# New costs for the planner that orders the engines of an attention and two feed-forward layers

## The chip, the core and the metric

One NeuronCore of a Trainium2 chip runs the whole program; nothing is shared with other cores. The metric is the device time of one execution in microseconds (us). The kernel before takes 1226.68 us, the median of three executions (1225.52 to 1226.89).

## What is computed

```python
q_s = softmax(q, axis=-1);  k_s = softmax(k, axis=2)     # 4 x 8 heads x 576 x 64
kv  = einsum('bhsd,bhse->bhde', k_s, v)
x   = einsum('bhsd,bhde->bhse', q_s, kv)                 # then 2304 tokens x 512
h   = x @ w_in                                           # 512 x 2048
x   = (h * clip(h + 3, 0, 6) / 6) @ w_out                # 2048 x 512
p   = domain_probs / (domain_probs.sum(-1) + 1e-9)       # 4 experts
out = sum over e of p[:, e] * (relu(x @ w1[e]) @ w2[e])  # 512 x 1024 x 512
```

Inputs and output are float32.

## The kernel before

**Attention.** There are four batches. `k_part` (lines 384 to 433) treats two heads at a time: K is loaded (L386) and V (L388), VectorE takes the maximum (L417), ScalarE the exponential (L419), TensorE transposes (L398) and multiplies (L405), VectorE scales the result into `bd` (L412, L413). `q_part` treats 128 tokens of Q at a time: load (L444), maximum (L462), a subtraction (`each`, recorded at L315), exponential (L465), sum (L467), reciprocal (L471), a multiplication (L315 again), four transposes on TensorE (L460). `x_part` makes the attention's result: a product (L499) into one of the PSUM places "pa", a copy of it, rounded to fp32r, by ScalarE (L502), and the rest of that rounding by VectorE (L506). There are 32 such products and 32 such splits, eight a batch. From the second batch on only two "pa" places may be used.

**First layer.** 96 steps, each with twelve matmuls of 384 columns (L606 to L608, called here a first product) and twelve more (L650, a second product). A step pairs one block of 384 tokens with one of 16 chunks of the hidden layer. Its result goes through ScalarE (L620), VectorE (L623), ScalarE (L629) and a subtraction that leaves the low half (L315, on VectorE or GpSimd). The chunks' weights arrive as float64 (L544); `w_half` turns each half of a chunk into a high and a low fp32r half: VectorE (L554), ScalarE (L558), VectorE twice (L560, L563), ScalarE (L566), VectorE (L569), a product of 512 columns (L315, `o6`), ScalarE (L574), a subtraction of 512 columns (L315, `o8`).

**Later layers.** `w_prepare` (L799 and L315, 256 columns) forms the second feed-forward layer's seven combinations of each weight block while the first layer runs and stores them to DRAM. Then come the three units of 768 tokens: the first at L1062 and L1184, the other two at L941 and L1257 with evictions at L1306.

**What sets the order.** The kernel emits nothing directly. Each operation is an `Op` with the engines that may run it and a cost on each; `Plan.order` (from line 155) plays the program through with these costs, engine by engine, takes at each time the ready operation with the smallest key, and the operations are emitted in the order of the starts so found. Each engine then runs its own list strictly in order on the chip. So a cost in the program changes no instruction; it changes where the instruction stands in its engine's list, and, where two engines may run it, on which. L315 is the helper `tt`, through which VectorE (DVE) and GpSimd (POOL) run the same `tensor_tensor`:

```python
def tt(o, out, a, b, op):
    on(o).tensor_tensor(out=out, in0=a, in1=b, op=op)
def rather_pool(n):
    return {"Pool": pool_(n), "DVE": dve2(n)}
```

The first engine of such a pair is preferred; the other takes the operation if the first would end it `PREFER = 1.5` us or more from now (for VectorE as the first: later than the other would).

Of the kernel before, what the change touches and what calls it, by code (L numbers as in the profile page):

```python
# [20 lines left out]
DM = H * D  # L21
# [3 lines left out]
P = 128  # L25
# [62 lines left out]


def dve2(n):  # L90

    return 0.155 + 1.6e-3 * n


def act(n):
    return 0.165 + 0.87e-3 * n


def pool_(n):
    return 0.2 + 2.4e-3 * n  # L100
# [5 lines left out]

# [19 lines left out]
class Plan:  # L126
# [23 lines left out]
    @staticmethod  # L150
    def after(e, x):
        to = next(iter(x.eng))
        return 0.0 if to == e else hop(e, to)

    def order(self):
# [5 lines left out]
        for o in reversed(self.ops):  # L161
            if o.due is None:
                e = next(iter(o.eng))
                o.due = min((x.due - self.after(e, x) for x in o.then), default=1e6) - o.eng[e]
# [4 lines left out]
        clock = dict.fromkeys(engines, 0.0)  # L169
# [10 lines left out]
        done, t, total = [], 0.0, len(self.ops)  # L180
        while len(done) < total:
            moved = False
            soon = [c for c in clock.values() if c > t]
            for e in engines:
# [3 lines left out]
                for o in cand[e]:  # L188
# [4 lines left out]
                    if best is not None and o.key >= best.key:  # L193
                        continue
# [41 lines left out]
def tile_kernel(ctx: ExitStack, tc: tile.TileContext, q, kt, v, w64, w, p, out):  # L236
# [147 lines left out]
    def k_part(b, j):  # L384
        pst = {}
        ld = load("kt", {"SP": 0.85}, lambda o: nc.sync.dma_start(out=KT[o.place], in_=kt[b, j]),  # L386
                  (), ("kt", lambda n: b < 3 or n < 3))
        vld = load("v", {"SP": 0.95}, lambda o: nc.sync.dma_start(out=V[o.place], in_=v[b, j]),  # L388
# [28 lines left out]
        o1 = add({"DVE": 0.74}, lambda o: nc.vector.tensor_reduce(  # L417
            out=nms[ld.place], in_=t(), axis=AX.X, op=ALU.max, negate=True), [ld])
        o2 = add({"ACT": 0.77}, lambda o: nc.scalar.activation(  # L419
            out=t(), in_=t(), func=AF.Exp, bias=nms[ld.place]), [o1])  # L420
        to = load("ek", {"": 0.0}, lambda o: None, [o1], ("ek", lambda n: n < 2 or b == 0))
        o3 = add({"PE": 0.85}, lambda o: turn(o, range(4)), [o2, to], pa_place(b == 0))
        o5 = add({"PE": 0.2}, lambda o: turn(o, [4]), [o3], pa_place(b == 0), [("kt", ld)])
        o4 = add({"ACT": 0.6}, lambda o: nc.scalar.activation(
            out=EK[to.place][:, 0:4 * P], in_=pst[o3], func=AF.Copy), [o3], None, [("pa", o3)])
        o6 = add({"ACT": 0.26, "DVE": 0.28}, lambda o: copy(
            o, EK[to.place][:D, 4 * P:5 * P], pst[o5][:D, :]), [o5, o4], None, [("pa", o5)])
        o7 = add({"PE": 1.2}, kv, [o6, vld] + bd_readers[j], pa_place(b == 0),
                 [("ek", to), ("v", vld)])
        o8 = add({"DVE": 0.5}, scale, [o7], None, [("pa", o7)])  # L430
# [10 lines left out]
    def q_part(b, t):  # L441
        n = min(P, S - t * P)
        pst = {}
        ld = load("q", {"SP": 0.75}, lambda o: nc.sync.dma_start(  # L444
# [17 lines left out]
        o1 = add({"DVE": 0.67}, lambda o: nc.vector.tensor_reduce(  # L462
            out=m(), in_=heads(x()), axis=AX.X, op=ALU.max), [ld])
        o2 = add({"Pool": 1.2, "DVE": 0.7}, lambda o: each(o, ALU.subtract), [o1])
        o3 = add({"ACT": 0.62}, lambda o: nc.scalar.activation(  # L465
            out=x(), in_=x(), func=AF.Exp), [o2])
        o4 = add({"DVE": 0.67}, lambda o: nc.vector.tensor_reduce(  # L467
            out=m(), in_=heads(x()), axis=AX.X, op=ALU.add), [o3])
        o4 = add({"ACT": 0.2}, lambda o: nc.scalar.activation(
            out=m(), in_=m(), func=AF.Copy, bias=EPS), [o4])  # L470
        o4 = add({"DVE": 0.18}, lambda o: nc.vector.reciprocal(m(), m()), [o4])  # L471
        o5 = add({"Pool": 1.25, "DVE": 0.7}, lambda o: each(o, ALU.mult), [o4])
        before = [o for s0, s1, bb, o in qt_readers if s0 < t * P + n and s1 > t * P and bb < b]
        o6 = add({"PE": 0.8}, turn, [o5] + before, pa_place(b == 0 and t < 2), [("q", ld)])
        q_done[b, t] = add({"ACT": 0.6}, lambda o: nc.scalar.activation(
# [8 lines left out]
    def x_part(b, s0, n):  # L484
# [4 lines left out]
        for j in range(NPAIR):  # L489
            if (bi, j) not in x0_place:  # L490
                def new(o, j=j):
                    x0[bi, j] = x_tile(o.place, f"x0_{bi}{j}")

                x0_place[bi, j] = load("x", {"": 0.0}, new, (), ("x", None))
# [1008 lines left out]
```

## Time and profile before

| | |
|---|---|
| median of three executions | 1226.68 us |
| span of the profiled execution (the page has no other time of it) | 1225.2 us, 1.5 below the median |
| TensorE (PE) busy | 1196.2 us, 98% |
| TensorE weight loads (PEld) | 1148.9 us, 94% |
| VectorE (DVE) | 881.0 us, 72%, 1486 instructions |
| ScalarE (ACT) | 596.4 us, 49% |
| GpSimd (POOL) | 670.7 us, 55%, 656 instructions |
| HBM | 194 GB/s over the span |

The busy share of TensorE is the time in which some matmul is in flight, so it says when the engine stood still, and not whether it ran at its full rate. That is told by how many matmuls it gets through and by the granted clock.

### The profile page before, as it was taken

The page shows a single profiled execution, that of the slowest core. Times are in us where ns is not written, and L with a number is a line of the kernel's source. Part 1 is how long each engine was busy: PE and PEld are TensorE (multiplying, and loading weights), DVE is VectorE, ACT ScalarE, POOL GpSimd, SP SyncE. Part 2 cuts the span into 40 slices and gives each one's busy share as a digit, 9 for nine tenths or more (in the row PEclk, how much of TensorE's full clock was granted, in tenths as well). Part 3 has the DMA queues.
Part 4 walks back from the last instruction along what each step waited for, and adds up shares of the span by engine and source line. Part 5 has one row for each costly group of instructions (what it writes and reads, how often), then busy time and mean ns, then how long its engine had stood idle before and what let it go on. Part 6 is the DMA issues. An engine that isn't in the chain of part 4 may idle for free.

```text
span 1225.2 us, 21162 instructions
## 1 busy us (share of the span) xinstructions
PE 1196.2 (98%) x7296; PEld 1148.9 (94%) x7296; DVE 881.0 (72%) x1486; ACT 596.4 (49%) x1256; POOL 670.7 (55%) x656
## 2 busy tenths in 40 slices
PE   5799999999999999999999999999999999999998
PEld 4698999999999999988888899999999999999998
DVE  7889732888984866765665586777777877777775
ACT  6677433655654644544444444444444444444441
POOL 3767234756776865756666544444444654444442
PEclk9899999999999999999999999999999999999999
DMA  8433212345565653655555457787877788877771
GB/s 299 152 99 136 75 69 96 107 160 157 187 226 179 224 190 121 206 190 189 189 189 183 170 173 251 265 251 248 252 248 248 239 295 248 250 249 243 246 252 53
DMA packets 125275, 238.99 MB, mean 195 GB/s; under 512 B 14064, under 2 KB 14064, under 8 KB 125168
## 3 DMA queue, kind: packets, MB, share of 16 engines
q1 hardware_dynamic: 125168, 237.64, 59.1%
q8 instruction: 58, 0.95, 0.3%
q14 instruction: 49, 0.40, 0.1%
HBM read 174.14 MB, written 63.44 MB: 194 GB/s over the span
## 4 chain that ended last, share of the span: by engine, by line
PE 84%; DVE 5%; POOL 4%; issue 2%; DMA 2%; ACT 1%; SPq 0%; DVEq 0%; POOLq 0%; ACTq 0%
PE ps L1257 19%; PE ps L941 18%; PE ps L650 12%; PE ps L1184 11%; PE ps L1062 10%; PE ps L608 4%; PE ps L607 4%; PE ps L606 4%; POOL w L315 1%; PE ps L405 1%; POOL st L315 1%; DMA st<-in_w_dram 1%; DMA vd<-w 1%; PE ps L499 1%; DVE acc L1306 1%
## 5 line engine op out<-in xcount | busy, mean ns | idle before, releaser
L941 PE MATMUL ps<-x,w 128*128 128x384 f32 x1344 | 264.4, 335 | 0.0
L1257 PE MATMUL ps<-w,g 128*128 128x256 f32 x1737 | 244.2, 283 | 2.0 <-DVE acc L1306 1.8
L1257 PEld LDWEIGHTS ps<-w,g 128*128 128x128 f32 x1737 | 228.5, 189 | 6.0 <-DVE acc L1306 6.0
L941 PEld LDWEIGHTS ps<-x,w 128*128 128x128 f32 x1344 | 227.2, 189 | 0.8
L650 PE MATMUL ps<-g,w 128*128 128x384 f32 x1152 | 225.3, 340 | 1.8 <-ACT g L629 0.8
L650 PEld LDWEIGHTS ps<-g,w 128*128 128x128 f32 x1152 | 199.8, 188 | 7.0 <-DVE g L315 2.2
L1306 DVE SCALAR_TENSOR_TENSOR acc<-ps,pt,acc 128x256 f32<-128x256 f32 x312 | 143.4, 480 | 79.5 <-PE ps L1257 77.5
L315 POOL TENSOR_TENSOR w<-st,w 128x256 fp32r<-128x256 f32 (+1 forms) x133 | 137.3, 1048 | 99.6 <-ACT w L899 59.4
L315 POOL TENSOR_TENSOR g<-t,g 128x384 fp32r<-128x384 f32 x98 | 107.8, 1106 | 116.5 <-ACT g L964 114.3
L1184 PE MATMUL ps<-w,g 128*128 128x512 f32 x576 | 148.9, 394 | 0.0
L608 PE MATMUL ps<-x,w 128*128 128x384 f32 x384 | 129.4, 337 | 2.4 <-POOL w L315 1.8
L1062 PE MATMUL ps<-x,w 128*128 128x384 f32 x672 | 131.0, 335 | 0.0
L606 PE MATMUL ps<-x,w 128*128 128x384 f32 x384 | 129.1, 336 | 0.0
L607 PE MATMUL ps<-x,w 128*128 128x384 f32 x384 | 129.0, 336 | 0.0
L1062 PEld LDWEIGHTS ps<-x,w 128*128 128x128 f32 x672 | 119.4, 188 | 7.8
L1184 PEld LDWEIGHTS ps<-w,g 128*128 128x128 f32 x576 | 106.6, 188 | 16.7
L623 DVE SCALAR_TENSOR_TENSOR r<-r,ps 128x384 f32<-128x384 f32 x96 | 52.6, 549 | 76.5 <-ACT r L620 75.8
L620 ACT ACTIVATE r<-ps,three 128x384 f32<-128x384 f32 x96 | 55.7, 580 | 105.0 <-PE ps L608 103.0
L964 ACT ACTIVATE g<-t 128x384 fp32r<-128x384 f32 x145 | 73.8, 521 | 43.0 <-DVE t L1006 18.0
L949 ACT ACTIVATE t<-ps 128x384 f32<-128x384 f32 x90 | 44.1, 490 | 69.8 <-PE ps L941 69.6
L315 POOL TENSOR_TENSOR st<-st 128x256 f32<-128x256 f32 (+1 forms) x56 | 63.2, 1131 | 24.1 <-DVE st L569 20.3
L608 PEld LDWEIGHTS ps<-x,w 128*128 128x128 f32 x384 | 72.6, 189 | 3.3 <-POOL w L315 2.6
(173 smaller groups left out, 1932.0 us busy)
## 6 DMA issues: line engine op xcount, KB each, us to landing
w<-wd SPq DMA_DIRECT2D x224, 256.0 KB, 3.2
w<-vd SPq DMA_DIRECT2D x224, 256.0 KB, 3.6
vd<-w SPq DMA_DIRECT2D x112, 256.0 KB, 2.4
wd<-w SPq DMA_DIRECT2D x112, 256.0 KB, 3.3
st<-in_w_dram SPq DMA_DIRECT2D x64, 256.0 KB, 3.9
st<-in_w_dram SPq DMA_DIRECT2D x30, 512.0 KB, 3.9
raw<-in_w_dram SPq DMA_DIRECT2D x32, 256.0 KB, 3.5
out_dram<-acc SPq DMA_DIRECT2D x18, 256.0 KB, 2.3
```

Of the source, the lines that this page charges most:

```text
L315: on(o).tensor_tensor(out=out, in0=a, in1=b, op=op)
L606: nc.tensor.matmul(pst[0], lhsT=hi, rhs=a, start=(k == 0), stop=False)
L607: nc.tensor.matmul(pst[0], lhsT=hi, rhs=b, start=False, stop=False)
L608: nc.tensor.matmul(pst[0], lhsT=lo, rhs=a, start=False, stop=(k == NK - 1))
L620: nc.scalar.activation(out=pst["r"], in_=pst[0], func=AF.Relu, bias=three)
L650: nc.tensor.matmul(y, lhsT=l, rhs=r, start=(s["start"] and not low and m == 0), stop=(s["stop"] and bool(low)))
L941: nc.tensor.matmul(bank(i), lhsT=l, rhs=r, start=(opens and k == 0 and m == 0), stop=(k == 1 and m == 2), skip_group_check=not opens)
L964: nc.scalar.activation(out=made[i][0][:, :n], in_=at(src), func=AF.Relu if raw else AF.Copy)
L1062: nc.tensor.matmul(bank(i), lhsT=l, rhs=r, start=(opens and k == 0 and m == 0), stop=(k == 1 and m == 2), skip_group_check=not opens)
L1184: nc.tensor.matmul(y, lhsT=l, rhs=rr, start=opens and x == 0, stop=closes and x == len(seq) - 1)
L1257: nc.tensor.matmul(y, lhsT=l, rhs=r, start=clears and x == 0, stop=x == len(seq) - 1, skip_group_check=True)
L1306: o1 = add({"DVE": dve(half) + 0.03}, lambda o: nc.vector.scalar_tensor_tensor(out=a, in0=y, scalar=s, in1=a, op0=ALU.mult, op1=ALU.add), ...
```

## The change

Every cost that the planner uses is replaced. A cost is now a `Cost`: the time for which the engine is taken (the number itself), the time after which the result is there (`lat`), and whether the operation needs the SBUF port that VectorE and GpSimd share (`port`). The planner keeps one clock for this port: an operation with `port` is not started while another holds it. Loads cost their size over 400 KB per us and land 1.9 us later, instead of a fixed time each and 2.5 us. The hops between engines become shorter (0.05 to 0.09 us in place of 0.16 to 0.27). All engines start at 5.6 us, the load queue at 2.0 us.

```diff
-START, FIRST, COLD = 18.0, 0.75, 0.0
+START, FIRST, BEGIN = 18.0, 2.0, 5.6
+HOPS = {"PE": 0.06, "ACT": 0.05, "DVE": 0.05, "Pool": 0.09, "SP": 0.05, "": 0.0}
+LAND = 1.9
+class Cost(float):
+    def __new__(cls, occ, late=0.08, port=False):
+        x = float.__new__(cls, occ)
+        x.lat, x.port = occ + late, port
+        return x
 def hop(a, b):
-    if b == "SP":
-        return 2.0
-    return 0.27 if b == "PE" else 0.2 if a == "PE" else 2.5 if a == "SP" else 0.16
+    return LAND if a == "SP" else HOPS[b]
 def dve(n):
-    return 0.155 + 1.05e-3 * n
+    return Cost(0.064 + n / 960)
+def dvep(n):
+    return Cost(0.124 + n / 960)
 def dve2(n):
-    return 0.155 + 1.6e-3 * n
+    return Cost(0.064 + n / 960, 0.08, True)
 def act(n):
-    return 0.165 + 0.87e-3 * n
+    return Cost(0.092 + n / 1200, 0.1)
 def pool_(n):
-    return 0.2 + 2.4e-3 * n
+    return Cost(0.16 + 2.1e-3 * n if n < 600 else 3.25e-3 * n, 0.05, True)
+def dma(n):
+    return Cost(n / 400.0, 0.0)
...
@@ Plan.order
-        clock = dict.fromkeys(engines, 0.0)
+        clock = dict.fromkeys(engines, BEGIN)
...
+                    if o.eng[e].port and port > t:
+                        soon.append(port)
+                        continue
...
-                cold = 2 if e == "PE" and o.start < COLD else 1
-                clock[e] = o.start + o.eng[e] * cold
-                o.end = clock[e]
+                clock[e] = o.start + o.eng[e]
+                o.end = o.start + o.eng[e].lat
+                if o.eng[e].port:
+                    port = clock[e]
...
@@ w_half (the other operations likewise)
-        o1 = add({"DVE": 0.6}, lambda o: nc.vector.tensor_scalar(
+        o1 = add({"DVE": Cost(0.33, 0.08, True)}, lambda o: nc.vector.tensor_scalar(
...
-        o6 = add({"Pool": 1.35, "DVE": 0.7}, lambda o: tt(
+        o6 = add({"Pool": pool_(DM), "DVE": dve2(DM)}, lambda o: tt(
```

No instruction is added or taken out. By the lists of the built programs, 133 of the `tensor_tensor` instructions of L315 go from VectorE to GpSimd (58 of 256 columns, 47 of 384, 28 of 512) and 9 of 768 columns go the other way. TensorE's list differs up to the end of the attention and over some 190 matmuls at the end of the first layer; between and after these it is the same, row for row.

The next three places are those at which the lists differ and TensorE waits or is waited for. Names with a number are tiles; the changed file's lines are 32 further down, so that L347 there is L315 here.

TensorE, from the end of the first product of the first step (the first of all; `x_03` is the last of its operands, `ident` marks transposes, `qt` and `bd` the attention's products L499, `vs` and `spare_110` hold V, `g` is the operand of a second product). Before:

```order
L608 MATMUL ps_115<-x_03_143,w_0_1_145 128x384
L398 MATMUL ps_118<-ident,spare_109 64x128
L460 MATMUL ps_117<-ident,qs_97 128x128 x4
L460 MATMUL ps_118<-ident,qs_98 128x128 x4
L499 MATMUL ps_117<-qt,bd_91 128x192
L499 MATMUL ps_118<-qt,bd_89 128x192
L650 MATMUL ps_119<-g,w_1_0_146 128x384
L650 MATMUL ps_119<-g,w_1_1_147 128x384
```

After:

```order
L640 MATMUL ps_115<-x_03_152,w_0_1_148 128x384
L492 MATMUL ps_118<-ident,qs_97 128x128 x4
L492 MATMUL ps_117<-ident,qs_98 128x128 x4
L531 MATMUL ps_118<-qt,bd_91 128x192
L531 MATMUL ps_117<-qt,bd_89 128x192
L437 MATMUL ps_118<-vs_95,acc 128x129 x5
L531 MATMUL ps_117<-qt,bd_92 128x192
L531 MATMUL ps_118<-qt,bd_91 128x192
L437 MATMUL ps_117<-vs_96,acc 128x129 x5
L531 MATMUL ps_118<-qt,bd_90 128x192
```

The second product of the first step stood behind two products of the attention; now most of the second batch, and a part of the third, stands between.

VectorE, from the maximum or split that follows the first batch's last wide split to the first L569 (the last VectorE step of the first half chunk, whose operand is `st_113`). Before:

```order
L506 TENSOR_TENSOR x_03_143<-ps_122,x_03_143 128x384
L462 TENSOR_REDUCE qm_105<-qs_98 128x8
L417 TENSOR_REDUCE nm_100<-acc 128x1
L417 TENSOR_REDUCE nm_101<-acc 128x1
L506 TENSOR_TENSOR x_10_156<-ps_118,x_10_156 128x192
L417 TENSOR_REDUCE nm_102<-acc 128x1
L417 TENSOR_REDUCE nm_103<-spare_109 128x1
L560 SCALAR_TENSOR_TENSOR st_114<-st_114 128x512
L554 TENSOR_SCALAR acc<-acc 128x512
L467 TENSOR_REDUCE qm_104<-qs_97 128x8
L467 TENSOR_REDUCE qm_105<-qs_98 128x8
L569 SCALAR_TENSOR_TENSOR st_113<-st_113 128x512
```

After:

```order
L538 TENSOR_TENSOR x_03_152<-ps_122,x_03_152 128x384
L344 COPY acc<-ps_117 64x128
L494 TENSOR_REDUCE qm_106<-qs_99 128x8
L601 SCALAR_TENSOR_TENSOR st_113<-st_113 128x512
L592 SCALAR_TENSOR_TENSOR st_114<-st_114 128x512
```

The four maxima of K (L417) now stand further up, and steps of the next half chunks (`st_114`, `acc`) further down, so that the first L569 comes eight rows sooner behind the split.

GpSimd, around the same half chunk's last two operations (`st_113` is `o6`, `w_0_1_145` or `w_0_1_148` is `o8`; `qs` and `spare` are Q). Before:

```order
L315 TENSOR_TENSOR st_113<-st_113 128x512
L315 TENSOR_TENSOR qs_97<-qs_97,qm_104 128x512
L315 TENSOR_TENSOR qs_98<-qs_98,qm_105 128x512
L315 TENSOR_TENSOR w_0_1_145<-st_113,w_0_0_144 128x512
L315 TENSOR_TENSOR st_114<-st_114 128x512
L315 TENSOR_TENSOR w_1_1_147<-st_114,w_1_0_146 128x512
```

After:

```order
L347 TENSOR_TENSOR st_113<-st_113 128x512
L347 TENSOR_TENSOR qs_99<-qs_99,qm_106 128x512
L347 TENSOR_TENSOR qs_97<-qs_97,qm_104 128x512
L347 TENSOR_TENSOR w_0_1_148<-st_113,w_0_0_146 128x512
L347 TENSOR_TENSOR qs_98<-qs_98,qm_105 128x512
L347 TENSOR_TENSOR spare_111<-spare_111,qm_107 128x512
```

Between `o6` and `o8` stand two operations of Q in both; the second half's pair, which followed at once, now stands behind the rest of the second batch's Q.

The load queue's first thirteen loads are the same. After them the second batch's K comes ahead of its Q.

## Rows read from the trace of the kernel before

**Rows 1.** The page: the span.

```profile
span 1225.2 us, 21162 instructions
```

**Rows 2.** Windows by stage: stretch, its length, busy us and (instructions) by engine, clock, DMA share, GB/s.

```profile
0.00:66.00 66.00, 46.50 (x240) 39.22 (x241) 53.12 (x108) 41.20 (x87) 38.26 (x38) 0.90 0.66 217
66.00:150.00 84.00, 82.85 (x512) 76.87 (x511) 72.60 (x144) 55.61 (x116) 43.85 (x34) 1.00 0.33 107
...
225.00:350.00 125.00, 124.18 (x711) 122.61 (x710) 113.33 (x163) 71.67 (x143) 83.03 (x77) 1.00 0.51 165
...
730.00:1200.00 470.00, 468.75 (x3256) 463.06 (x3255) 349.67 (x625) 204.01 (x416) 224.62 (x208) 1.00 0.78 248
```

**Rows 3.** Timeline of PE: start us, length us, instruction, [idle before <-releaser].

```profile
14.52 0.60 PE L398 MATMUL ps<-ident,acc 128*128 128x128 f32 x4
14.96 0.60 PE L398 MATMUL ps<-ident,spare 128*128 128x128 f32 x4
...
17.06 1.28 PE L405 MATMUL ps<-spare,acc 128*128 128x129 f32 x10
18.17 1.28 PE L405 MATMUL ps<-vs,acc 128*128 128x129 f32 x10
...
23.06 2.85 PE L499 MATMUL ps<-qt,bd 128*128 128x384 f32 x8 [0.69 <-ACT qt L475]
25.75 0.99 PE L460 MATMUL ps<-ident,spare 128*128 128x128 f32 x8
...
41.73 0.45 PE L606 MATMUL ps<-x,w 128*128 128x384 f32 x1
...
163.20 0.81 PE L499 MATMUL ps<-qt,bd 128*128 128x384 f32 x2
```

**Rows 4.** The chain that ended last: start us, length us, piece; one second product.

```profile
166.61 2.08 PE ps L650 x12
```

**Rows 5.** Windows of 2 and 7.2 us at the start, as in rows 2.

```profile
28.00:30.00 2.00, 0.23 (x2) 0.03 (x1) 2.00 (x5) 1.57 (x4) 1.04 (x1) 1.00 0.82 264
33.40:40.60 7.20, 6.22 (x26) 5.38 (x26) 4.15 (x12) 3.40 (x10) 5.16 (x4) 0.50 0.54 167
```

**Rows 6.** Timeline of DVE, columns as in rows 3.

```profile
26.21 1.47 DVE L506 TENSOR_TENSOR x<-ps,x 128x384 fp32r<-128x384 f32 x3
...
33.22 0.68 DVE L569 SCALAR_TENSOR_TENSOR st<-st 128x512 f32<-128x512 uint32 x1
...
43.22 0.41 DVE L554 TENSOR_SCALAR st<-st 128x512 int32<-128x512 int32 x1
43.55 0.70 DVE L569 SCALAR_TENSOR_TENSOR acc<-acc 128x512 f32<-128x512 uint32 x1
...
48.44 1.53 DVE L563 TENSOR_SCALAR st<-st 128x512 int32<-128x512 int32 x1
...
55.29 0.68 DVE L462 TENSOR_REDUCE qm<-spare 128x8 f32<-128x512 f32 x1
55.88 0.35 DVE L506 TENSOR_TENSOR x<-ps,x 128x192 fp32r<-128x192 f32 x1
...
78.90 1.01 DVE L506 TENSOR_TENSOR x<-ps,x 128x384 fp32r<-128x384 f32 x2
```

**Rows 7.** Timeline of POOL, columns as in rows 3.

```profile
48.20 1.49 POOL L315 TENSOR_TENSOR w<-acc,w 128x512 fp32r<-128x512 f32 x1
...
61.13 1.31 POOL L315 TENSOR_TENSOR st<-st 128x512 f32<-128x512 f32 x1
...
169.42 0.74 POOL L315 TENSOR_TENSOR w<-raw,w 128x256 fp32r<-128x256 f32 x1
```

**Rows 8.** Groups of DVE from 225 to 350 us: xcount | busy us, mean ns | idle before.

```profile
L315 DVE TENSOR_TENSOR w<-st,w 128x512 fp32r<-128x512 f32 x5 | 6.9, 1384 | 1.1 <-ACT w L574 0.9
L315 DVE TENSOR_TENSOR w<-wtmp,w 128x256 fp32r<-128x256 f32 x7 | 6.3, 907 | 0.3 <-ACT w L799 0.3
L315 DVE TENSOR_TENSOR st<-st 128x512 f32<-128x512 f32 x3 | 3.9, 1305 | 0.0
```

More of the change, by code (lines that the diff above doesn't have):

```diff
@@ L152, in after @@
         to = next(iter(x.eng))
-        return 0.0 if to == e else hop(e, to)
+        if to == e and e in ("PE", "SP"):
+            return -0.165 if e == "PE" else 0.0
+        return hop(e, to)
     def order(self):
@@ L163, in order @@
                 e = next(iter(o.eng))
-                o.due = min((x.due - self.after(e, x) for x in o.then), default=1e6) - o.eng[e]
+                o.due = min((x.due - self.after(e, x) for x in o.then), default=1e6) - o.eng[e].lat
             if o.key is None:
@@ L179, in order @@
                 open_(o)
-        done, t, total = [], 0.0, len(self.ops)
+        done, t, total, port = [], 0.0, len(self.ops), 0.0
         while len(done) < total:
@@ L492, in new @@
                     x0[bi, j] = x_tile(o.place, f"x0_{bi}{j}")
-                x0_place[bi, j] = load("x", {"": 0.0}, new, (), ("x", None))
+                x0_place[bi, j] = load("x", NONE, new, (), ("x", None))
             pst = {}
@@ L507, in low @@
                                         in1=x[:, at:at + n].bitcast(F32), op=ALU.subtract)
[L509 removed]
+            o1 = add({"PE": pes(0.013 + 1.667e-3 * n)}, product, deps + [kv_done[b, j], x0_place[bi, j]],
                      pa_place(b == 0 and s0 == 0))
@@ L524, in new @@
             store[key] = w_tile(o.place, "w_" + "_".join(str(x) for x in key))
-        return load(kind, {"": 0.0}, new, (), (kind, None))
+        return load(kind, NONE, new, (), (kind, None))
     w0, w_done, w_place = {}, {}, {}
@@ L575, in w_half @@
             out=w0[c, i, 0], in_=t(F32), func=AF.Copy), [o6] + space)
-        o8 = add({"Pool": 1.35, "DVE": 0.7}, lambda o: half_sub(
+        o8 = add({"Pool": pool_(DM), "DVE": dve2(DM)}, lambda o: half_sub(
             o, w0[c, i, 1], t(F32), w0[c, i, 0]), [o7], None, [("wt", o1)])
@@ L610, in h_part @@
         deps = x_done[bi] if s["first"] else []
-        o0 = add({"PE": 12 * pe(n)}, product, deps + w_done[c][:1] + h_before, ("ph", None),
+        o0 = add({"PE": pes(12 * pe(n))}, product, deps + w_done[c][:1] + h_before, ("ph", None),
                  key=i - 1.0, due=s["due"])
@@ L910, in main_pe @@
     def main_pe(cost, fn, deps, take=None, give=()):
-        o = add({"PE": cost}, fn, deps + main["last"], take, give, due=main["due"])
+        o = add({"PE": pes(cost)}, fn, deps + main["last"], take, give, due=main["due"])
         o.key = o.due
@@ L1148, in low @@
                     op0=ALU.max, op1=ALU.subtract)
-            o2 = add({"DVE": dve(n)}, low, [o1], None, [("t", src)])
+            o2 = add({"DVE": dve2(n)}, low, [o1], None, [("t", src)])
             made[key] += [o1, o2, pl]
@@ L1319, in shares @@
     def shares():
-        ld = add({"SP": 0.6}, lambda o: nc.sync.dma_start(out=pt, in_=p))
+        ld = add({"SP": dma(36)}, lambda o: nc.sync.dma_start(out=pt, in_=p))
         def normal(o):
@@ L1330, in normal @@
             )
-        norm.append(add({"DVE": 1.0}, normal, [ld]))
+        norm.append(add({"DVE": Cost(1.0)}, normal, [ld]))
     for b in range(B):
@@ L1429, in tile_kernel @@
         if u == 0:
-            add({"": 0.0}, lambda o: None, stage0, None, [("xt", i) for i in range(2)])
-            add({"": 0.0}, g_of_stage, stage0, None, [("g", 200), ("g", 201)])
+            add(NONE, lambda o: None, stage0, None, [("xt", i) for i in range(2)])
+            add(NONE, g_of_stage, stage0, None, [("g", 200), ("g", 201)])
         if u + 1 < len(UNITS):
```

132 lines of the change are left out of this document (68 added, 64 removed).

## The prediction

> **What bounds the kernel now.** I read the page first, then windows by stage, then the timelines of TensorE (PE), VectorE (DVE) and GpSimd (POOL) in the first 165 us. The span is 1225.2 us [rows 1], 1.5 below the median of the runs, 1226.7. The windows [rows 2] show two kernels: up to 66 us PE is in use for 46.5 of 66 us at a mean granted clock of 0.90, and DVE for 53.1; from 66 us on PE never stands still for more than about one us in a hundred. So all that a new order can win at once lies in the first stretch, and the later stretches are a list of matmuls at their full rate that the change leaves as it is.
>
> To say how much lies there I compare PE's clock time with the work that it has done by then, at full rate. The rates: a transpose 0.11 us (four in 0.44, from 14.52 to 14.96), the five matmuls of one K and V product 1.11 (17.06 to 18.17), a product of the attention of 384 columns 0.67 (two records of 0.336, from 23.06 to 25.75), one of 192 columns half of that [rows 3], twelve matmuls of the first layer 2.08 [rows 4]. The attention as a whole is 160 x 0.11 + 16 x 1.11 + 16 x 0.67 + 16 x 0.34 = 51.6 us.
>
> - The first first-layer product starts at 41.73 us [rows 3]; ahead of it lie 60 transposes, six K and V products and six of the attention's, 16.7 us. PE is 25 us behind.
> - The last product of the attention starts at 163.20 [rows 3]; ahead of it in PE's list lie the attention less this product, 50.9, and 441 first-layer matmuls, 76.4: 127.3 us. PE is 35.9 us behind. Since PE is idle for only 1.2 us from 66 to 150 at a clock of 1.00 [rows 2], nearly all of this was lost before 66.
>
> What holds PE there is DVE. Back to back its instructions take less than their records say: a reduction 0.59 (55.29 to 55.88), an L554 0.33 (43.22 to 43.55), a wide split 0.47 [rows 6]. By such times, 0.66 for a maximum of K and 0.60 for L560 and L569, I add up DVE's list: 17.8 us up to the fourth split, 24.1 up to the first L569, 52.9 up to the sixteenth split. They end at 27.68, 33.90 and 79.91 [rows 6]. So DVE is 9.9, 9.8 and 27.0 us later than its bare work: some 10 us of start and waits for loads, and 17 more later on. Where those go the rows show: an L554 or L563 that takes 0.41 alone takes 1.53 at 48.44, while GpSimd is in the middle of an operation (48.20, 1.49 long, which takes 1.31 elsewhere) [rows 6, 7]. Each of the two engines makes the other wait. 38 of the 128 DVE instructions up to the sixteenth split are of this kind.
>
> **The change part by part.** *Engines.* 133 `tensor_tensor` go from DVE to POOL and nine of 768 columns come back. On POOL one takes 1.31 us (512 columns) or 0.74 (256) alone [rows 7]. In the first stretch this cover is there: POOL is in use for 38.3 of 66 us [rows 2].
>
> *DVE's list.* Up to the sixteenth split it now holds 116 instructions, 46.1 us by the same times: twelve more reductions and maxima, seven fewer evictions, and 17 instead of 38 that contend for the port. Up to the first L569 it holds 20.5 us instead of 24.1. With the same 9.8 on top this L569 ends at 30.3 instead of 33.9, and the first first-layer product can start some 4 to 6 us sooner, at about 36: on POOL the same two Q operations stand between the half chunk's two.
>
> *PE's list.* Ahead of the second first product stood 18.2 us of attention and now stand 29.5, so that the attention comes earlier and fewer products of the first layer are there to fill its waits. Up to the second first product PE now has 94 transposes, ten K and V products, 16 of the attention's products and two twelves: 10.3 + 11.1 + 8.1 + 4.2 = 33.7 us. It stands behind the sixteenth split: the last product's place must be free, then two K and V products and four transposes follow, 2.7 us, of which some 1.0 passes while ScalarE and DVE still drain that product. So it starts 1.7 us after the sixteenth split ends.
>
> *The unknown* is how late DVE then is against its 46.1 us. Low end: 9.8, as at the first L569, nothing being added. High end: 27.0, as now. Between the first L569 and the sixteenth split the 17.2 us were added over 28 instructions of the contending kind, 0.61 each; 12 are left there, 7.3 us, which makes 17.1. I take 15, since part of the 17.2 was DVE idling behind first-layer products that no longer stand there (eight evictions, now one). Then the split ends at 61.1, the second first product starts at 62.8, and PE is 62.8 - 33.7 = 29.1 us behind. From there to the attention's end DVE has 41.3 us of bare work against 54.7 of PE's, so I add only 1.5 us, about the idle time of 66 to 150 now. PE ends the attention 30.6 us behind, not 35.9.
>
> *Loads.* Their number and the first thirteen are the same; the second batch's K before its Q agrees with DVE's list, so I cost it at nothing. If a load were late there DVE would stand with it; bounds are zero and the 2 to 3 us between issue and landing that the early rows leave.
>
> *After the attention.* PE's list is the same but for a swap at the end of the first layer. PE's own idle time there is 0.8 us in 225 to 350 and 1.3 in 730 to 1200 [rows 2]: that much can be won, and I take zero.
>
> **Sum:** 1225.2 - 35.9 + 30.6 = 1219.9 us of span, and with the 1.5 around it **1221.4 us**.
>
> **A rule that speaks against it.** Where the trace has both engines at work, the second to come waits for all of the first [rows 6, 7], and an operation holds the other engine off longer on POOL (0.74 or 1.31) than DVE's own time for it. From 225 to 350 us, DVE is in use for 113.3 of 125 and POOL for 83.0 [rows 2]. Five L315 of 512 columns into `w`, three into `st` and seven of 256 columns out of `wtmp` run on DVE there [rows 8]; with three single ones, eight of 512 and ten of 256 go to POOL. On DVE they hold the port for about 8 x 0.60 + 10 x 0.33 = 8.1 us, on POOL for 8 x 1.31 + 10 x 0.74 = 17.9: 9.8 us more of a port that is in use nearly all the time. The Trainium skill ("SBUF — State Buffer", section "Who interferes with whom") says that the two share one pair of ports under an exclusive lock, and ("Perfetto Trace Analysis", section "Optimizing Scalar/DVE Operations") that moving work between these two therefore might not help. By that rule the gain would be lost here, which is the second rival; the trace agrees with the lock, and whether moving helps, no row of it shows.
>
> **The rivals.**
> 1. *The wait changes its owner (slower).* DVE stays 27.0 us late at the sixteenth split: with fewer first-layer products between, PE idles, and after the idle stretch at 28 to 30 us its granted clock stood at 0.50 from 33.4 to 40.6 [rows 5]; the same now falls on the longer run of attention between the first two steps, and DVE waits for K and V products that take twice as long. Then the second first product starts at 74.8, PE is 41.1 behind, 42.6 at the end: 6.7 more than now, 1233.4 us. The point from which this decides is 66.5 us for the end of the sixteenth split. Against it: fewer contending instructions. Chance 0.14.
> 2. *The port takes it back (no change).* The gain of 5.3 us at the start holds, but the 9.8 us more of port time in 225 to 350 push the weight chunks late, and PE waits before L608 and L650. The chunks still have some slack, so half or so would reach PE: 1226 us, from 1224 to 1230. Against it: the attention ends 40 us of PE's list earlier, so the second layer's weights, which use the same port, can begin earlier and leave room. Chance 0.20.
> 3. *Nearly all contention goes (faster still).* DVE is only 9.8 us late at the sixteenth split: PE is 23.9 behind, 25.4 at the end, 10.5 less than now, 1216.2; with the 2.1 us of later idle time 1214. Speaking for it: the new costs are the chip's own (0.33 for an L554, 0.60 for an L569, 0.70 for 256 columns on POOL), and an order that keeps port operations apart is what they aim at. Chance 0.16.
>
> That the change does not do what it says can be left out: the lists show it.
>
> **How the numbers follow.** The forecast, 0.50, gives 1221.4, from 1218 to 1225 as DVE's lateness lies between 12 and 19. About 0.2% (2.5 us) is what a measurement of this kernel can tell from no change: faster means below 1224.2, slower above 1229.1. Faster: 0.46 of the forecast's 0.50 and rival 3's 0.16, and 0.02 of rival 2: 0.64. Within 0.2%: the remaining 0.04, and 0.14 of rival 2: 0.18. Slower: rival 1 with 0.14 and the last 0.04 of rival 2: 0.18. The range is 1213 to 1230: it takes in rival 3, the forecast and rival 2, and leaves out most of rival 1 and the far side of rival 3.
>
> **What would show it.** Right: in the changed kernel's timeline the first L569 (there L601) ends near 30 us, the first first-layer product starts near 36, the sixteenth split (there L538) ends near 61, the second first product starts near 63, and the last product of the attention starts about 30 us after its 88 us of work, near 118; behind 150 us the windows read as now. The contending DVE instructions take 0.4 to 0.7 more often than 1.5. Wrong: a sixteenth split after 66.5 us with a clock of 0.50 in the stretch before it (rival 1); PE idle for more than 5 us between 150 and 500 with L608 or L650 released by POOL (rival 2); or a start as before and a gain that comes from elsewhere.

## The result and the profile after

The changed kernel takes 1236.01 us (median of four executions, 1232.90 to 1237.48), the kernel before 1226.13 beside it: a ratio of 1.0073, 95% interval 1.0055 to 1.0091. Slower by 9.9 us, where 5.3 faster was forecast; the time lies outside the range.

The page and the windows of the changed kernel, the latter with the columns of [rows 2]; the fourth window is new and covers the stretch in which most of the loss arose:

```profile
span 1232.9 us, 21178 instructions
```

```profile
0.00:66.00 66.00, 43.80 (x235) 33.47 (x236) 51.77 (x117) 44.44 (x98) 37.94 (x41) 0.91 0.67 220
66.00:150.00 84.00, 82.17 (x497) 76.73 (x497) 62.67 (x126) 55.83 (x119) 58.91 (x53) 0.99 0.37 120
225.00:350.00 125.00, 120.45 (x673) 115.50 (x672) 94.37 (x149) 67.50 (x134) 84.92 (x78) 1.00 0.43 141
240.00:420.00 180.00, 174.61 (x979) 168.37 (x979) 116.83 (x190) 95.41 (x200) 131.16 (x141) 1.00 0.52 177
730.00:1200.00 470.00, 468.82 (x3241) 462.92 (x3241) 329.33 (x585) 208.87 (x421) 263.88 (x246) 1.00 0.78 253
```

The same window of the kernel before:

```profile
240.00:420.00 180.00, 178.59 (x1021) 176.34 (x1020) 144.19 (x212) 96.63 (x205) 122.28 (x127) 1.00 0.54 178
```

From 730 us on PE's columns read alike, as forecast. Up to 66 us PE is in use for 2.7 us less than in [rows 2], and from 240 to 420 us, where it hardly ever stood still, it now gets through 42 matmuls fewer. DVE is in use for 27 us less there and POOL for only 9 more: neither is short of time. So it is not work that holds PE, but waiting. The groups of [rows 8] are gone from DVE; on POOL, in the same stretch (225 to 350 us), their like now read:

```profile
L347 POOL TENSOR_TENSOR st<-st 128x512 f32<-128x512 f32 x16 | 23.8, 1496 | 26.7 <-DVE st L601 26.7
L347 POOL TENSOR_TENSOR w<-st,w 128x512 fp32r<-128x512 f32 x16 | 22.8, 1432 | 3.0 <-ACT w L606 2.9
```

One takes some 1.45 us, and before the first kind POOL stands idle for 26.7 us in all.

The measure below is the prediction's own: how far PE is behind, its clock time less the full-rate time of the matmuls ahead in its list. Before, it is 36.1 us behind at 240 us and 39.6 at 420; in the changed kernel 38.8 and 49.6. From 420 us on the change loses 2.3 us less than the kernel before, over several places that I did not follow. That is 2.7 + 7.3 - 2.3 = 7.7 us, the difference of the two spans (1232.9 and 1225.2; the changed kernel's profiled execution took 1234.68, 1.3 less than its median).

**Where PE waits from 240 to 420 us.** What ScalarE (ACT) waits for there, summed by what released it (us in total, times, longest us). Before:

```profile
ACT w L799 <- DMA vd<-w: 1.8, 2, 1.6
```

Changed:

```profile
ACT w L831 <- DMA vd<-w: 33.2, 31, 4.1
```

L831 (L799 before) is `w_prepare`'s rounding of a weight block. It writes into a place whose last contents must first have been stored to DRAM (`vd<-w`). The wait for such a store, 1.8 us in all before, is 33.2 now, in 31 pieces. One of them, in the changed kernel's chain of waits (start us, us, what), in ACT's timeline and in PE's (columns as in [rows 3]):

```profile
285.16 5.72 DMA vd<-w
...
291.29 0.52 ACT g L661
```

```profile
286.25 0.58 ACT L652 ACTIVATE r<-ps,three 128x384 f32<-128x384 f32 x1 [0.84 <-PE ps L640]
290.97 0.42 ACT L831 ACTIVATE w<-wtmp 128x256 fp32r<-128x256 f32 x1 [4.13 <-DMA vd<-w]
291.29 0.51 ACT L661 ACTIVATE g<-r 128x384 fp32r<-128x384 f32 x1
```

```profile
291.85 2.35 PE L682 MATMUL ps<-g,w 128*128 128x384 f32 x12 [1.47 <-ACT g L661]
```

The store is issued at 285.16 and is done 5.72 us later. The plan counted 0.64 + 1.9 = 2.54 us for it, so it put L831 into ACT's list where its place would be free, and behind it the `g` of L661, which PE needs. Each engine runs its list strictly in order, so `g` and PE wait with a weight block that nobody needs yet.

The two do not stand in another order than before: an L799 stood directly ahead of 15 of the 42 `g` of this stretch, an L831 stands directly ahead of 14 of 41 now. What went is the room behind the store. Counted from the end of the operation whose result it stores, the plan before allowed 2.0 + 0.9 + 2.5 = 5.4 us until the place is free, the changed one 0.05 + 0.64 + 1.9 = 2.59. The stores themselves did not become slower: from issue to landing they take a median of 2.3 us (2.0 to 5.7), and took 2.8 before (2.0 to 6.1).

What PE waits for there, and what VectorE (DVE) waits for at the first step of a half chunk. Before:

```profile
PE ps L650 <- ACT g L629: 0.6, 1, 0.6
DVE st L554 <- DMA st<-in_w_dram: 1.8, 1, 1.8
```

Changed:

```profile
PE ps L682 <- ACT g L661: 4.1, 7, 1.5
DVE st L586 <- DMA st<-in_w_dram: 8.8, 5, 3.0
```

Of PE's seven waits for `g`, three (at 291.85, 382.07 and 403.83, 2.2 of the 4.1 us) follow an L831 that stood for a store. At one (246.86) `g` itself waited for DVE. Ahead of the other three (271.49, 281.78 and 338.79, 1.3 us) ACT stood for DVE with a step of the weights' preparation, L590 or L598, as here for the one at 281.78:

```profile
280.66 0.66 ACT L598 ACTIVATE st<-st 128x512 f32<-128x512 int32 x1 [2.36 <-DVE st L595]
281.22 0.51 ACT L661 ACTIVATE g<-r 128x384 fp32r<-128x384 f32 x1
```

That preparation begins with L586, which stands 8.8 us for loads of weights. These are transfers too, but whether they made those waits is not shown. PE's idle time is 180 - 174.6 = 5.4 of the 10.8 us that it falls further behind; the rest are late starts that a busy share does not show, since a matmul of the first layer is in flight for 0.33 us and the next starts after 0.17.

**The first 66 us.** VectorE's timeline, and PE's, in the changed kernel:

```profile
28.79 0.69 DVE L494 TENSOR_REDUCE qm<-qs 128x8 f32<-128x512 f32 x1 [1.92 <-DMA qs<-in_q_dram]
29.39 0.68 DVE L601 SCALAR_TENSOR_TENSOR st<-st 128x512 f32<-128x512 uint32 x1
...
57.72 1.78 DVE L592 SCALAR_TENSOR_TENSOR st<-st 128x512 int32<-128x512 int32 x1
59.42 1.26 DVE L595 TENSOR_SCALAR acc<-acc 128x512 int32<-128x512 int32 x1
60.60 1.01 DVE L538 TENSOR_TENSOR x<-ps,x 128x384 fp32r<-128x384 f32 x2
...
64.69 0.56 DVE L538 TENSOR_TENSOR x<-ps,x 128x384 fp32r<-128x384 f32 x1 [0.72 <-ACT x L534]
```

```profile
31.29 1.30 PE L430 MATMUL ps<-ident,acc 128*128 128x128 f32 x5 [2.98 <-DVE bd L445]
...
33.91 2.36 PE L437 MATMUL ps<-spare,acc 128*128 128x129 f32 x10
...
37.51 0.42 PE L638 MATMUL ps<-x,w 128*128 128x384 f32 x1
...
61.20 2.93 PE L531 MATMUL ps<-qt,bd 128*128 128x384 f32 x4 [3.32 <-DVE x L538]
...
68.28 0.42 PE L638 MATMUL ps<-x,w 128*128 128x384 f32 x1
...
126.52 1.13 PE L531 MATMUL ps<-qt,bd 128*128 128x384 f32 x3
```

The first first-layer product starts at 37.51 instead of 41.73 [rows 3], so the gain forecast there came. Before that a load is late: DVE stands for 1.92 us before a maximum of Q, and with it all that is behind, the scaling of `bd` (L445) for which PE then stands 2.98 us among it. Behind that pause a K and V product takes 2.36 us where one took 1.28 [rows 3]: the granted clock was 0.50, the lower of its two levels, from 33.9 to 36.3. From 33.4 to 40.6 it was 0.78 (0.50 before, [rows 5]). At 57 to 61 us contending steps of later half chunks (1.78 and 1.26 us) stand ahead of the splits for which PE waits 3.32. By the second first product, at 68.28, the gain is spent; the row with the attention's last product starts at 126.52 instead of 163.20, but the forecast had it near 118. What DVE waits for up to 66 us in the changed kernel, and the one row of the kernel before that answers to it, in the same view:

```profile
DVE qm L494 <- DMA qs<-in_q_dram: 5.9, 4, 2.0
...
DVE qm L494 <- DMA spare<-in_q_dram: 1.8, 1, 1.8
```

```profile
DVE qm L462 <- DMA qs<-in_q_dram: 2.8, 2, 2.0
```

7.7 us of waiting for Q, against 2.8; with the old transfers (e1 below) it is 2.7.

**The plan against the trace.** The planner writes into each operation when it would start. The trace's start less the planned one, for the VectorE instruction next after each time (the planned starts are numbers of the kernel's program, not measurements):

```
us in the trace     23     37     65    160    300    420
before            +2.2   +2.0   +4.2   -0.9   +0.2   +2.2
change            +1.4   +5.8  +11.0  +13.7  +18.8  +23.8
```

The kernel before is planned with costs that are mostly a little too long, and the trace keeps up with it. The change is planned with the engines' bare times, and falls ever further behind its own plan. In itself that loses nothing. It says that the order was chosen for a program that does not happen.

### The profile page after: what moved, and what is told of

Its sections match the earlier page's. It is cut to its first block, busy times and chain, and to the rows that moved or that the text cites. A ratio compares the mean times of both kernels' runs of the same rounds, so it can differ in the third digit from the quotient of the medians.

```text
span 1232.9 us, 21178 instructions
## 1 busy us (share of the span) xinstructions
PE 1197.6 (97%) x7296; PEld 1146.5 (93%) x7296; DVE 779.1 (63%) x1362; ACT 600.7 (49%) x1256; POOL 757.7 (61%) x780
## 4 chain that ended last, share of the span: by engine, by line
PE 80%; POOL 6%; DMA 5%; DVE 4%; issue 3%; ACT 1%; SPq 0%; DVEq 0%; POOLq 0%; ACTq 0%
PE ps L1289 19%; PE ps L973 19%; PE ps L1216 11%; PE ps L1094 9%; PE ps L682 9%; POOL w L347 3%; PE ps L638 3%; PE ps L640 3%; PE ps L639 3%; DMA vd<-w 3%; POOL st L347 1%; DMA qs<-in_q_dram 1%; PE ps L437 1%; POOL wtmp L347 1%; PE ps L531 1%
## 5 line engine op out<-in xcount | busy, mean ns | idle before, releaser
L347 POOL TENSOR_TENSOR w<-st,w 128x256 fp32r<-128x256 f32 (+1 forms) x174 | 173.8, 1016 | 114.7 <-ACT w L931 76.8
L973 PEld LDWEIGHTS ps<-x,w 128*128 128x128 f32 x1344 | 227.2, 189 | 0.8
L347 POOL TENSOR_TENSOR g<-t,g 128x384 fp32r<-128x384 f32 x128 | 140.9, 1109 | 124.8 <-ACT g L996 108.4
L1094 PEld LDWEIGHTS ps<-x,w 128*128 128x128 f32 x672 | 119.4, 188 | 7.8
L347 POOL TENSOR_TENSOR st<-st 128x256 f32<-128x256 f32 (+1 forms) x66 | 74.4, 1131 | 48.6 <-DVE st L601 45.3
L996 ACT ACTIVATE g<-t 128x384 fp32r<-128x384 f32 x143 | 74.6, 525 | 59.3 <-DVE t L1038 21.6
L347 POOL TENSOR_TENSOR t<-t 128x384 f32<-128x384 f32 x47 | 47.9, 1020 | 45.3 <-ACT t L981 38.9
L981 ACT ACTIVATE t<-ps 128x384 f32<-128x384 f32 x104 | 50.3, 484 | 52.1 <-PE ps L973 51.5
```

Source lines behind the costliest of these rows:

```text
L973: nc.tensor.matmul(bank(i), lhsT=l, rhs=r, start=(opens and k == 0 and m == 0), stop=(k == 1 and m == 2), skip_group_check=not opens)
L996: nc.scalar.activation(out=made[i][0][:, :n], in_=at(src), func=AF.Relu if raw else AF.Copy)
L1094: nc.tensor.matmul(bank(i), lhsT=l, rhs=r, start=(opens and k == 0 and m == 0), stop=(k == 1 and m == 2), skip_group_check=not opens)
```

## The experiments

Theory T (transfers): the change costs transfers too short, and the lists put instructions that need a load or a store ahead of those that PE needs. Theory P (port), the prediction's second rival: the rule for the port and the operations that moved to GpSimd cost the time. A later question was whether the runs scatter by where the order happens to fall. Eighteen runs; "lost" is how much further PE falls behind from 240 to 420 us, "stores" what ACT waits for `vd<-w` there:

| run | us | ratio to before, 95% interval | PE behind at 42 / at 150 us | lost | stores |
|---|---|---|---|---|---|
| before | 1226.1 | | 25.2 / 35.9 | 3.5 | 1.8 |
| change | 1236.0 | 1.0073 (1.0055 to 1.0091) | 21.6 / 38.7 | 10.8 | 33.2 |
| e1 old transfers | 1225.8 | 0.9998 (0.9989 to 1.0007) | 20.8 / 36.6 | 4.0 | 3.0 |
| e2 weight load 2.0 | 1229.0 | 1.0022 (1.0013 to 1.0032) | 22.8 / 38.8 | 4.8 | 23.9 |
| e3 no port rule | 1263.7 | 1.0312 (1.0295 to 1.0329) | 21.6 / 40.9 | 31.4 | 25.5 |
| e4 e1 and e3 | 1248.5 | 1.0191 (1.0175 to 1.0208) | 22.3 / 43.0 | 16.1 | 9.0 |
| e5 before, new transfers | 1245.2 | 1.0151 (1.0135 to 1.0167) | 27.2 / 40.8 | 16.9 | 27.1 |
| e6 e1, slack on port | 1239.8 | 1.0104 (1.0088 to 1.0120) | 24.0 / 38.4 | 6.3 | 1.2 |
| e7 e1, old hops | 1221.8 | 0.9966 (0.9953 to 0.9979) | 22.9 / 34.9 | 1.3 | 2.1 |
| e8 e1, weight load 2.0 | 1221.8 | 0.9961 (0.9945 to 0.9976) | 20.1 / 34.6 | 2.0 | 3.5 |
| e9 e7 and e8 | 1227.7 | 1.0013 (1.0004 to 1.0023) | 24.1 / 40.3 | 1.3 | 0 |
| e10 change, old hops | 1226.2 | 1.0000 (0.9988 to 1.0012) | 20.3 / 36.8 | 4.9 | 16.2 |
| e11 change, 1% longer | 1232.0 | 1.0043 (1.0031 to 1.0054) | 22.2 / 38.9 | 5.8 | 23.5 |
| e12 change, old landing | 1229.8 | 1.0023 (1.0011 to 1.0035) | 25.1 / 42.4 | 3.2 | 3.5 |
| e13 change, 1% shorter | 1236.2 | 1.0083 (1.0067 to 1.0100) | 21.6 / 39.3 | 11.3 | 31.1 |
| e14 e8, 1% longer | 1221.1 | 0.9960 (0.9947 to 0.9973) | 20.2 / 34.0 | 1.9 | 3.1 |
| e15 e7, 1% longer | 1222.3 | 0.9971 (0.9959 to 0.9982) | 21.5 / 33.3 | 2.1 | 3.3 |
| e16 before, 1% longer | 1225.3 | 0.9997 (0.9988 to 1.0006) | 25.1 / 34.6 | 2.9 | 0.4 |
| e17 before, more on GpSimd | 1227.2 | 1.0008 (0.9999 to 1.0018) | 22.6 / 38.0 | 2.7 | 2.1 |
| e18 e8, less on GpSimd | 1223.9 | 0.9981 (0.9972 to 0.9991) | 24.8 / 36.2 | 2.9 | 2.2 |

### Transfers or port

**e1**: the changed kernel, its transfers costed as before (nearly: each transfer of 256 KB at 0.9 us, where a load of Q had 0.75 and some others 0.95).

```diff
-HOPS = {..., "SP": 0.05, "": 0.0}
-LAND = 1.9
+HOPS = {..., "SP": 2.0, "": 0.0}
+LAND = 2.5
+FIXED = {288: 0.85, 322: 0.95, 256: 0.9, 512: 1.5, 128: 0.75}
-    return Cost(n / 400.0, 0.0)
+    return Cost(FIXED[n], 0.0) if n in FIXED else Cost(n / 400.0, 0.0)
```

> The changed kernel with its transfers costed as before: a fixed time for each (0.85 for K, 0.95 for V, 0.9 for 256 KB, 1.5 for 512 KB), 2.5 us to landing, 2.0 us from an engine to the load queue. Theory T (transfers): in the changed kernel ScalarE waits 33.2 us in 240 to 420 us for stores whose places the plan believed free (1.8 before), VectorE 8.8 for loads (1.8 before), and PE loses 10.9 us there against 3.5; with the old costs that falls to about 4, the ramp gains 1 to 3, and the kernel takes 1225 to 1229 us. Theory P (port): the port rule and the 133 operations that it sends to GpSimd cause the loss; they stay, so the time stays at 1234 to 1238 us.

**e2**: one number, the load of half a chunk's float64 weights.

```diff
-        ld = load("raw", {"SP": dma(512)}, ...
+        ld = load("raw", {"SP": dma(800)}, ...
```

> The changed kernel with one number changed: a 512 KB load of float64 weights costs 2.0 us of the load queue instead of 1.28 (in the changed kernel's first 30 us such a load held the stream 1.1 to 2.2 us). Theory T: the 2 us for which VectorE stands at 28.8 us before a Q that lands late go, and part of the later waits: 1229 to 1233 us. Theory P: 1234 to 1238 us.

**e3**: the planner without the rule for the port; **e4**: e1 and e3 together.

```diff
-                    if o.eng[e].port and port > t:
-                        soon.append(port)
-                        continue
```

> The changed kernel without the rule that an operation waits for the port (three lines of the planner); its costs stay. VectorE then has 1431 of the operations and GpSimd 676, nearly as before (1462 and 647). Theory T: transfers are costed as in the change, so most of the loss stays: 1232 to 1238 us. Theory P: the 240 to 420 us stretch loses about 4 us as before and the time is 1224 to 1229 us.

> Both: the transfers costed as before and no port rule; what is left of the change are the short times of the engines and the short hops. If either theory is all, this equals the better of the two runs within 2 us. If the engines' short times themselves (no slack at all) cause the loss, it stays at 1233 us or more.

T holds and P falls. With the old transfers (e1) the kernel takes what it took before, 10.2 us less than the change, although the port rule and the 771 operations on GpSimd stay. ACT's wait in 240 to 420 us, and the window, in e1:

```profile
ACT w L834 <- DMA vd<-w: 3.0, 4, 1.6
```

```profile
240.00:420.00 180.00, 178.06 (x1018) 175.76 (x1017) 120.93 (x195) 94.20 (x199) 126.42 (x135) 1.00 0.49 166
```

The one number of e2 brings 7.0 us (3 to 7 against the three samples of the change's beliefs, below): PE loses 4.8 us from 240 to 420 instead of 10.8, though ACT still waits 23.9 us for stores. As one of these samples (e11) loses 5.8 there, what e2 brings in that stretch is not told apart from the fall of the order. The 2 us at 28.8 us that e2 was to remove did not go either: DVE still waits 5.9 us for Q, and PE is 38.8 behind at 150.

e3 came out above both of its ranges. Taking the rule away gives nothing back, it costs 27.6 us more, and 22.7 with the old transfers (e4 against e1). e4 so meets its third case, that the engines' short times cost by themselves; but in e1 they stand beside the rule and cost nothing. Here bare times on the engines are only usable together with the rule.

**e5**: the opposite, the kernel before with the change's transfers alone (`/ 400.0` for each fixed time, 1.9 for 2.5, 0.05 for 2.0).

> The kernel before with only the transfers costed as in the change (size over 400 KB per us, 1.9 us to landing, 0.05 us to the load queue). Theory T in its strong form (a plan that believes transfers too short loses by that alone): PE loses 7 to 10 us between 240 and 420 us instead of 3.5, and 1 to 2 more in the ramp: 1231 to 1237 us. Weak form (the dearer engine times of the kernel before leave slack that takes the lateness up): 1225 to 1229 us.

18.6 us slower than the kernel before beside it, above even the range of the strong form and worse than the whole change, with the same picture: ACT's wait for stores (before 1.8), and PE behind ACT's `g` over the same stretch:

```profile
ACT w L799 <- DMA vd<-w: 27.1, 28, 3.0
```

```profile
PE ps L650 <- ACT g L629: 8.3, 8, 1.6
```

So the strong form of T holds. The change as a whole, 1236.0, is 9.2 us better than its transfers alone: beside the new transfers the rest of it is a gain, while beside the old ones (e1 against the kernel before) it is worth nothing.

### How much room a plan needs

**e12** undoes landing and the hop to the load queue alone, **e10** the hops between the engines alone (about as before), both in the changed kernel. **e7** and **e8** add old hops, or 2.0 us for a weight load, to e1; **e9** both; **e6** adds a slack to each operation that takes the port.

```diff
 e12
-LAND = 1.9
+LAND = 2.5
-HOPS = {..., "SP": 0.05, "": 0.0}
+HOPS = {..., "SP": 2.0, "": 0.0}
 e7, e9, e10
-HOPS = {"PE": 0.06, "ACT": 0.05, "DVE": 0.05, "Pool": 0.09, ...
+HOPS = {"PE": 0.2, "ACT": 0.15, "DVE": 0.15, "Pool": 0.2, ...
 e8, e9
-FIXED = {..., 512: 1.5, 128: 0.75}
+FIXED = {..., 512: 2.0, 128: 0.75}
 e6
-    return Cost(0.064 + n / 960, 0.08, True)
+    return Cost(0.144 + n / 960, 0.08, True)
-    return Cost(0.16 + 2.1e-3 * n if n < 600 else 3.25e-3 * n, 0.05, True)
+    return Cost(0.26 + 2.1e-3 * n if n < 600 else 3.25e-3 * n, 0.05, True)
-        o1 = add({"DVE": Cost(0.33, 0.08, True)}, ...
+        o1 = add({"DVE": Cost(0.4, 0.08, True)}, ...
...
```

> The changed kernel with 2.5 instead of 1.9 us to landing and 2.0 instead of 0.05 us from an engine to the load queue; the loads keep 400 KB per us. Theory T, stores: ScalarE's 33.2 us of waiting for stores in 240 to 420 us falls under 10, the loss there from 10.8 to 5 to 7 us: 1228 to 1232 us. If the load time was all: 1234 to 1238 us.

> The changed kernel with hops of 0.15 to 0.2 us, its transfers left as they are. Theory T: the transfers still cost most of it, 1230 to 1235 us. If the lack of room between engines is a cause by itself: 1222 to 1228 us.

> The run with the old transfers, and hops between the engines of 0.15 to 0.2 us, about as before, instead of 0.05 to 0.09. Theory S: 1221 to 1225 us. Theory N: 1225 to 1229 us.

> The run with the old transfers, and 2.0 instead of 1.5 us for a 512 KB load of weights. If the weights' loads are still believed too short: 1222 to 1225 us; if 1.5 with 2.5 us to landing is long enough: 1225 to 1228 us.

> The run with the old transfers, with both steps that helped: 2.0 us for a 512 KB load and hops of 0.15 to 0.2 us. If the two gains are of different places they add up: 1217 to 1220 us. If both only take up the same lateness: 1221 to 1223 us.

> The run with the old transfers (1225.8 us), and a slack of 0.07 to 0.1 us on each operation that takes the port. Theory S (exact times leave no room for an engine that comes late, so a little room helps): the ramp and 240 to 300 us lose 1 to 4 us less, 1221 to 1225 us. Theory N (what the run with the old transfers still loses is not the plan's lack of room): 1225 to 1229 us.

Wherever the plan gets room for a transfer or between engines, PE loses 1.3 to 4.9 us from 240 to 420 instead of 10.8 (5.8 to 11.3 in the three samples). e12 does it by the stores, ACT's wait for them falling to 3.5 us; of its gain in the middle, 7.6 us, the first 150 us take 3.7 back. e10 does it though ACT waits 16.2; that a longer hop leaves `g` more time, so that the wait ends before PE stands, is my reading and not shown. e10 was forecast at 1230 to 1235 under T and took 1226.2, so the short hops are a cause beside the transfers, and the two overlap: either undone alone (e1, e10) gives all 10 us back, or 6 against the fastest of the three samples.

e7 and e8 beat both kernels, by 0.34 and 0.39% of the time before, 4.2 and 4.8 us. In e8 the two stretches read:

```profile
0.00:66.00 66.00, 46.98 (x246) 37.87 (x247) 54.93 (x121) 47.76 (x104) 41.12 (x44) 0.92 0.65 220
...
240.00:420.00 180.00, 178.81 (x1031) 178.20 (x1031) 127.35 (x194) 93.72 (x198) 129.31 (x137) 1.00 0.50 167
```

More room is not always better. e9, with both, lies at 1227.7, above both of its ranges: its middle is as good (1.3 us lost), but at 150 us PE is 40.3 us behind. e6 is worse than the change itself, 1239.8, with 6.3 us lost from 240 to 420 and more behind 490 us. I have not followed either further. So theory S of these expectations, that room as such helps, holds for transfers and hops one at a time and fails for the port's operations.

### Controls

A list of several thousand instructions changes in many rows with any cost. **e11** and **e13** are the change with transfers 1% longer and shorter, **e14**, **e15** and **e16** are e8, e7 and the kernel before with 1% longer ones.

```diff
 e11
-    return Cost(n / 400.0, 0.0)
+    return Cost(n / 396.0, 0.0)
-LAND = 1.9
+LAND = 1.92
 e13: 404.0 and 1.88
 e14: 2.02 for 2.0, 2.52 for 2.5
 e15, e16: 1.52 for 1.5, 2.52 for 2.5
```

> A control: the changed kernel with its transfers 1% longer (396 instead of 400 KB per us, 1.92 instead of 1.9 us to landing). It alters the order in many rows but no belief of the plan. Theory T: 1233 to 1239 us as the change. If the time follows from where the order happens to fall, it moves by 4 us or more, and differences of that size between other runs say little.

> A second control on the changed kernel: transfers 1% shorter (404 KB per us, 1.88 us to landing). If its time follows from what the plan believes: 1232 to 1238 us, all three above the kernel before by over 0.4%. If it follows from where the order happens to fall: anything from 1224 to 1240 us.

> A control on the run with the old transfers and 2.0 us for a weight load: 1% longer (2.02 us, 2.52 us to landing). Belief: 1220 to 1225 us, below the kernel before. Fall of the order: up to 1230 us.

> A control on the run with the old transfers and hops: 1% longer (1.52 us for a weight load, 2.52 us to landing). Belief: 1220 to 1225 us. Fall of the order: up to 1230 us.

> A control on the kernel before: 1.52 instead of 1.5 for a weight load, 2.52 instead of 2.5 us to landing. Belief: 1224 to 1229 us. Fall of the order: it may move by 4 us or more.

The change's beliefs give 1236.0, 1232.0 and 1236.2 us; those of the kernel before 1226.1 and 1225.3; e8's 1221.8 and 1221.1; e7's 1221.8 and 1222.3. So a time can move by 4 us by the fall of the order, and e11's 5.8 us lost (against 10.8 and 11.3) shows where. Differences of that size between single runs decide nothing. That the change is slower, and that e7 and e8 are faster, stands in every sample.

### The moved operations alone

**e17**: the kernel before, in which GpSimd gives up an operation later, so that 145 more run there (the change moves 124 net). **e18**: e8 with 73 given back.

```diff
-    PREFER = 1.5
+    PREFER = 2.5        (e17; e18: 1.0)
```

> The kernel before with PREFER 2.5 instead of 1.5 us, so that GpSimd gives up an operation later: 145 more on GpSimd (792 instead of 647; the change moves 124 net), nothing else altered. Theory P (the moved operations hold the port longer and delay the weights): PE loses 5 us more in 240 to 420 us, 1230 us or more. Theory T (the shift does not matter): 1223 to 1229 us.

> The run with the old transfers and 2.0 us for a weight load (1221.8 us), with PREFER 1.0 instead of 1.5 us: 73 operations go back from GpSimd to VectorE (698 instead of 771). Theory P: faster still, 1217 to 1220 us. Theory T: 1220 to 1225 us.

With the old transfers, moving them costs nothing that can be told from no change (1.0008, 0.9999 to 1.0018), and giving some back gains nothing. P is out in both directions there; beside the new transfers no run moves them alone.

## Why the prediction was wrong

- **What bounds the kernel, and the lists: right.** PE's full-rate work is the same, nothing is lost behind 420 us that was not lost before, and the early lists did what was said: the first L601 (L569 before) ends at 29.39 + 0.68 = 30.07 us (30.3 forecast), the first first-layer product starts at 37.51 (about 36). That the 9.8 us of lateness which I had kept for that first L601 came true was partly luck: DVE's idle time up to there grew from some 7 to some 9 us, the late Q among it, and the contention went.
- **"The unknown", DVE 15 us late at the sixteenth split: 19.1.** It ends at 65.25, not 61.1. Less contention came than the 15 us hold (5.2 above the 9.8): up to there the records of L586, L592, L595 and L601 exceed 0.41 and 0.68 us by 3.1 us in all, against 9.3 before (their old lines L554 to L569). What was mis-sized is DVE's idle time, for which I had kept the 9.8 us of the first L569; it is 14.8, as it was before (14.1).
- **"Loads ... I cost it at nothing": failed.** Waiting for Q alone rose from 2.8 to 7.7 us, more than the upper bound of 2 to 3. The order of the loads was looked at, not what the plan believed of their landing.
- **The second first product 1.7 us after that split, and "only 1.5 us" more up to the attention's end: 3.0 and 4.1.** PE is 68.28 - 33.7 = 34.6 behind there and 38.7 at the end. With the 4.1 us above these make the 8.1 us between 30.6 and 38.7. The three samples of the change's beliefs lie at 38.7 to 39.3; e7, e8 and their controls reach 33.3 to 34.9, the kernel before and its control 35.9 and 34.6. So of the 5.3 us that I priced for the start at most 2.6 were to be had, by orders other than the change's.
- **"After the attention ... I take zero": the largest failure.** The list of PE is the same there, but a list of PE says nothing of what ACT's list holds ahead of PE's operands. The change lowers three costs of a transfer: to reach the queue (2.0 to 0.05), to land (2.5 to 1.9), and in the queue (1.5 to 1.28 for a weight load, 0.9 to 0.64 for a store). The part-by-part account had engines, lists and loads, and no line for these; the description of the change names the hops of 0.16 to 0.27 and not the 2.0. They brought L831 to where its place is not yet free, ahead of a `g`, and PE lost 7.3 us more from 240 to 420. That the costs of transfers did it, e1 and e5 show from both sides; how the 7.3 divide between stores and loads of weights stays open.
- **Rival 1** named 66.5 us as its point; the split came at 65.25, and PE was 38.7, not 42.6 behind. The time, 1233.4, is near the result by another road.
- **Rival 2** named the right stretch and a wrong cause. Its sign, PE idle for over 5 us between 150 and 500, appeared (180 - 174.6 = 5.4 in 240 to 420 alone), but PE was released by ACT's `g` (4.1 us), not by POOL, and e1 and e17 clear the port. **Rival 3**'s hope, an order that keeps port operations apart, came for the contention (3.1 of 9.3 us left) and not for the time.
- **The rule from the Trainium skill** ("Perfetto Trace Analysis", section "Optimizing Scalar/DVE Operations"), that moving work between the two engines might not help: e17 agrees, 145 moved operations changed the time by 0.08%. The price that I worked out from rows beside it, 9.8 us more of the port, was not paid: with it in place and the old transfers e1 takes what the kernel before takes.

## What to carry to other kernels

Costs in a planner that writes fixed lists are not only estimates to be made exact: an operation planned too early blocks all that stands behind it on its engine. The old cost of 2.0 us from an engine to the load queue was no estimate that held, since in both traces a store is issued a median of 0.03 us after the operation ahead of it, and yet it was room for stores that land late. Room in a cost helped in e7, e8, e10 and e12 and not in e6 and e9, so it has to be tried. For each cost that a change lowers, ask which in-order list now holds a possibly late instruction ahead of what the bounding engine needs, above all for transfers, whose landing depends on what else is in the queue. And run the same beliefs with costs shifted by 1% before believing a difference of a few us.

## What the runs showed of the hardware

A transfer's time from issue to landing is not a matter of its own size alone. The issues of the changed kernel from 240 to 420 us (count, KB each, median us to landing), and two rows of the load queue's timeline (us of issue, length of the issue):

```profile
vd<-w SPq DMA_DIRECT2D x73, 256.0 KB, 2.3
st<-in_w_dram SPq DMA_DIRECT2D x14, 512.0 KB, 3.9
```

```profile
284.46 0.33 SPq L576 DMA_DIRECT2D st<-in_w_dram  x1
285.16 7.38 SPq L837 DMA_DIRECT2D vd<-w  x3
```

A weight load has a median of 3.9 us where the plan has 1.28 + 1.9 = 3.18. A store's median, 2.3, is even below the plan's 2.54; but the first store of 285.16, issued 0.7 us behind a weight load, took the 5.72 us of the chain above. I had not expected stores that are cheap by themselves to be late through the load ahead of them in the queue. It is so throughout the stretch: of the 72 stores issued in it, the 36 that were issued while a load was still under way landed after a median of 3.6 us (2.0 to 5.7), the other 36 after 2.0 (2.0 to 2.9). Before it was the same, 47 with a median of 3.3 and 27 with 2.0, under a plan that left more room. Nor did I expect so little from the port: the kernel with 145 operations more on GpSimd (e17) takes the same time within 0.2%.
